# A hand-fixed order of issue in place of a planner, and weight loads issued by ScalarE

## The chip, the core and the metric

The kernel runs on one core of a Trainium2 chip. The metric is the device time of that core in microseconds, lower being better. A core has five engines that run their own instruction streams in order: TensorE (PE) for matmuls, VectorE (DVE), ScalarE (ACT) and GpSimd (POOL) for elementwise work, and SyncE (SP), which here only starts DMA transfers. An engine waits only for the semaphores that its next instruction names. PSUM is the memory that TensorE writes into, in banks; SBUF is the memory that everything else works in.

## What is computed

First a linear attention with decay over 768 steps, for 4 batches of 8 heads of width 48, then a feed-forward layer on the 384 columns that the heads make together.

```
state = 0                                   # [B, H, 48, 48]
for t in range(768):
    cur   = (u * k[t]) outer v[t]
    y[t]  = r[t] @ (state + cur)
    state = w * state + k[t] outer v[t]

x   = y, heads joined to 384 columns        # 4 x 768 rows
xn  = (x - mean(x)) / sqrt(var(x) + 1e-6) * g_ln
out = x + relu(xn @ w_ch1) @ w_ch2          # 384 -> 1536 -> 384
```

## The kernel before

The rows are cut into 24 tiles of 128 (six to a batch). The recurrence is computed by chunks of 128 steps: inside a chunk as a masked matrix of scores, between chunks by a running state. A tile i goes through these steps, and the names below are those of the tasks in the code:

- loads: `k{i}`, `v{i}`, and `r{e}` for a pair of tiles, all from HBM;
- `sck{i}`, `scr{e}0`, `scr{e}1`: k and r multiplied by tables of powers of the decay (`Fk`, `Fr0`, `Fr1`);
- `TK{i}`, `TR{e}` on PE transpose them into the PSUM bank "tr"; `kT{i}`, `rT{i}` copy the results to SBUF; `vc{i}` casts v;
- `q{i}`, `cc{i}`, `cp{i}`, `Vb{i}`: the bonus term with u, as a factor on v;
- `at{i}` on PE gives the scores, `A{i}` on DVE masks them, `y{i}` on PE multiplies by v and adds what comes from the state;
- `kv{i}`, `S{i}`, `Z{i}`: the state for the next tile, which `WLZ` (a spread table of the decay over a chunk) multiplies;
- `x{i}`, `xn{i}`, `sq{i}`, `rs{e}`: the tile of x with its sum, centered, its squares, and one over the standard deviation;
- `ln{i}` (transposed on PE for tiles 0 to 7) and `lc{i}` (its copy to SBUF, or a DMA transpose from tile 8 on) give the transposed input of the feed-forward layer;
- `up{g}_{m}` on PE multiplies by w1 into one of two "hp" banks, `re{g}_{m}` applies relu; a group g is one tile for the first six and two tiles after that, with 3 or 6 ups;
- `dn{i}0` to `dn{i}2` on PE multiply by the three thirds of w2 into bank "o"; `ot{i}` scales and adds x; `st{i}` stores. The last tile is done in two halves of the columns (`dh`, `oh`, `sh`).

The weights come as three thirds each: `w1l0` to `w1l2` and `w2l0` to `w2l2`, 768 KB apiece, in float32. `w1s{n}{kc}` casts w1 and multiplies it by minus `g_ln` (the table `g_neg`, task `gn`); `w2s{n}{f}` casts w2. An up with m = 0, 1, 2 of a single-tile group needs the third with the same number, and so does a down third.

Every step is a task with an engine, sometimes with other engines that could do it (`alt`), the tasks that it needs, and the buffers that it takes and gives. The method `order` of the class `Planner` plays a list schedule: it keeps a clock for each engine, picks the task that can start first by its assumed costs and lags, breaks ties by priority, and picks the engine that would end it first. A table `SHIFT` changes priorities, earliest times and engines of 24 tasks by name. The instructions are emitted in the order that comes out, and each engine's stream has just that order. Where the plan foresees a gap on PE before the first down matmul, `keep_warm` fills it with matmuls of an identity matrix into a spare bank (line 285), whose results nobody reads.

In this kernel SP starts nearly all DMAs, the weights among them (`load_w1`, line 234, and `load_w2`, line 238). ACT starts the first v and six stores. DMAs started by SP share one hardware queue, those by ACT another. Each DMA signals on one of eight semaphores, and a DMA that is given a semaphore in use waits at its issue until the earlier DMA on it has landed.

Of the kernel before, what the change touches and what calls it, by code (L numbers as in the profile page):

```python
# [22 lines left out]
SHIFT = {  # L23
    "up9_0": (0.0, 94.5, ""), "S15": (-4.2, 0.0, ""), "cp14": (0.0, 81.3, ""), "ln5": (0.0, 43.7, ""),
    "re12_4": (0.0, 131.8, ""), "Vb2": (0.0, 25.0, ""), "dn52": (-5.3, 0.0, ""), "q19": (0.0, 103.6, ""),
    "xn16": (0.0, 0.0, "DVE"), "x17": (0.0, 99.3, ""), "sq15": (0.0, 89.8, ""), "sck3": (0.0, 18.7, ""),
    "dn32": (7.3, 0.0, ""), "y10": (0.0, 67.0, ""), "v13": (0.0, 52.8, ""), "TR2": (0.0, 27.7, ""),
    "w1l0": (0.0, 11.3, ""), "v9": (0.0, 40.3, ""), "re7_1": (0.0, 73.1, ""), "Vb19": (0.0, 107.1, ""),
    "rT5": (0.0, 0.0, "DVE"), "re13_1": (0.0, 0.0, "DVE"), "re9_1": (0.0, 0.0, "ACT"), "q21": (0.0, 114.6, ""),
}  # L30


class Planner:
# [12 lines left out]
    def add(self, name, eng, cost, fn, needs=(), takes=(), gives=(), pri=0, load=0.0, kind=None,  # L46
            alt=None, lands=1.9, after=0.0):

        t = dict(name=name, eng=eng, cost=cost, fn=fn, needs=list(needs), takes=list(takes),
                 gives=list(gives), pri=pri, load=load, kind=kind, alt=alt, lands=lands, end=None,
                 first=(eng, cost), after=after)
        self.tasks.append(t)
        assert name not in self.by_name, name
        if name in SHIFT:
            p, late, e = SHIFT[name]
            t["pri"], t["after"] = pri + p, max(after, late)
            for other in [t["first"]] + (alt or []):
                if other[0] == e:  # L60
                    t["first"], t["only"] = other, True
        self.by_name[name] = t

    def order(self, patience=0.0, spread=0.0, seed=0):


        rng = random.Random(seed)
        family = {t["name"]: t["name"].rstrip("0123456789_") for t in self.tasks}
        vary = {f: rng.uniform(-spread, spread) for f in sorted(set(family.values()))}
        for t in self.tasks:  # L70
            t["end"] = None
            t["eng"], t["cost"] = t["first"]
        free_at = {k: [0.0] * n for k, n in self.room.items()}
        held = {}
        eng_at = {e: 0.0 for e in self.LAG}
        eng_at["SP"], dma_at = 3.5, 5.9
        last_kind = None
        todo = list(self.tasks)
        out = []
        while todo:  # L80
            best = None
            for t in todo:
                data = t["after"]
                ok = True
                for n in t["needs"]:
                    d = self.by_name[n]
                    if d["end"] is None:
                        ok = False
                        break
                    lag = 0.0 if d["eng"] == t["eng"] else self.LAG[d["eng"]]  # L90
                    if d["load"] and d["lands"] == 1.9 and t["eng"] and d["start"] > SLT:
                        lag += SLK
                    data = max(data, d["end"] + lag)
                if not ok:
                    continue
                for b, _, _ in t["takes"]:
                    if not free_at[b]:
                        ok = False
                        break
                    data = max(data, min(free_at[b]))  # L100
                if not ok:
                    continue
                pri = t["pri"] + vary[family[t["name"]]]
                if t["kind"] is not None and t["kind"] == last_kind:
                    pri -= 0.5
                pick = None
                for eng, cost in [(t["eng"], t["cost"])] + ([] if "only" in t else t["alt"] or []):
                    ready = max(data, eng_at[eng] if eng else 0.0)
                    if t["load"]:
                        ready = max(ready, dma_at - (3.0 if eng == "SP" else 2.0))  # L110
                    if pick is None or ready + cost < pick[0]:
                        pick = (ready + cost, ready, eng, cost)
                key = (pick[1] - (patience * pri if pick[2] in ("DVE", "ACT", "POOL") else 0.0), -pri)
                if best is None or key < best[0]:
                    best = (key, t, pick)
            assert best is not None, [t["name"] for t in todo][:20]
            t, (_, t0, eng, cost) = best[1:]
            t["eng"], t["cost"] = eng, cost
            todo.remove(t)
            if t["kind"] is not None:  # L120
                last_kind = t["kind"]
            end = t0 + t["cost"]
            if t["eng"]:
                eng_at[t["eng"]] = end
            if t["load"]:
                dma_at = max(dma_at, end + 1.2) + t["load"]
                end = dma_at + t["lands"]
            t["start"], t["end"] = t0, end
            for b, owner, uses in t["takes"]:
                slots = free_at[b]  # L130
                slots.remove(min(slots))
                held[b, owner] = [uses, 0.0]
            for b, owner in t["gives"]:
                h = held[b, owner]
                h[0] -= 1
                h[1] = max(h[1], end)
                if h[0] == 0:
                    free_at[b].append(h[1] + self.LAG[t["eng"]])
            out.append(t)
        return out  # L140
# [3 lines left out]
def kernel(  # L144
# [82 lines left out]
    NW = 3  # L227
# [4 lines left out]
    def load_w1(n):  # L232
        w1_f[n] = wst.tile([P, CK, FW], FP32, name="wst")
        nc.sync.dma_start(out=w1_f[n][:], in_=w1_src[:, n])  # L234

    def load_w2(n):
        w2_f[n] = wst.tile([P, FK // NW, C], FP32, name="wst")
        nc.sync.dma_start(out=w2_f[n][:], in_=w2_src[:, n * FK // NW : (n + 1) * FK // NW])
# [44 lines left out]
    def keep_warm(n):  # L283
        for _ in range(n):
            nc.tensor.matmul(out=warm[:, :P], lhsT=ident[:], rhs=ident[:], start=True, stop=True)  # L285
# [318 lines left out]
    xT_t, hT_t, o_t, rs_t, sum_s = {}, {}, {}, {}, {}  # L604
# [8 lines left out]
    LNP = 8  # L613
    KP = 24
    SZ, QP = 6, 8
    ot_t = {}

    def ln_transposes(i):
        g, j = tile_group[i]
        if g not in xT_t:  # L620
            xT_t[g] = sb3.tile([P, CK, GW], BF16, name="xT")
        tp_t[i] = ps.tile([P, 2 * HP, P], BF16, name="tr")
        for kc in range(CK):
            nc.tensor.transpose(
                out=tp_t[i][:, kc, :], in_=xn_t[i][:, kc * P : (kc + 1) * P], identity=ident[:]
            )
# [7 lines left out]
    def ln_evacuate(i, eng):  # L634
        g, j = tile_group[i]
        (eng.copy if eng is nc.scalar else eng.tensor_copy)(out=xT_t[g][:, :, j * P : (j + 1) * P], in_=tp_t[i][:, :CK, :])
# [123 lines left out]
    for rank, (a, i) in enumerate(seq):  # L760
        pri = 50 - 0.1 * rank
        if a == "w1l":
            add(f"w1l{i}", "SP", 0.6, lambda i=i: load_w1(i), takes=[("wst", ("w1", i), CK)], pri=pri, load=2.1)
        elif a == "w2l":
            add(f"w2l{i}", "SP", 0.6,
# [15 lines left out]
    for i in range(NT):  # L781
# [5 lines left out]
        add(f"sckb{i}", "", 0.0, None, [], [("sck", i, 1 if last else 2)], pri=p0)  # L787
        add(f"sck{i}", "DVE", 0.7, lambda e, i=i: scale_k(i, e), [f"k{i}", "Fk", f"sckb{i}"], [], [("k", i)], pri=p0, after=35 + (i - 6) * PACE if i > 6 else 0.0,
            alt=[("POOL", 1.0)])
        if not half:  # L790
            add(f"scrb{e}", "", 0.0, None, [], [("scr", e, 1)], pri=p0)
# [58 lines left out]
        if i < LNP:  # L850
            add(f"ln{i}", "PE", 0.18, lambda i=i: ln_transposes(i), [f"xn{i}", f"xT{g}"], [("tr", ("l", i), 1)],
                [("xn", i)], pri=p0 + 2)
            add(f"lc{i}", "ACT", 0.5, lambda e, i=i: ln_evacuate(i, e), [f"ln{i}"], [], [("tr", ("l", i))], pri=p0 + 2, alt=[("DVE", 0.36)])
        else:
            add(f"lc{i}", "SP", 1.2, lambda i=i: ln_by_dma(i), [f"xn{i}", f"xT{g}"], [], [("xn", i)], pri=90, load=0.5, lands=3.0)
# [29 lines left out]
    pe_at = 6.3  # L885
    for t in plan.order():
        if t["eng"] == "PE":
            gap = t["start"] - pe_at - 0.1
            if gap > 0 and 0 not in o_t:
                keep_warm(int(gap / 0.057))  # L890
            pe_at = t["start"] + t["cost"]
        if t["fn"] is not None:
            if t["alt"] is not None:
                t["fn"]({"ACT": nc.scalar, "DVE": nc.vector, "POOL": nc.gpsimd, "SP": nc.sync}[t["eng"]])
            else:
                t["fn"]()
# [28 lines left out]
```

## Time and profile before

| | us |
|---|---|
| median of 11 runs | 157.91 |
| lowest and highest of them | 156.77, 159.8 |
| the profiled execution, own time | 157.31 |
| the profiled execution, span of the core | 155.2 |

The span runs from the first to the last instruction of the core in the trace; some 2 us of the measured time lie outside it. The profile page gives, for each engine, the time in which it was busy and its share of the span, then the span in 40 slices. It follows the chain of work that ended last back from the end, and prints its shares. Groups of instructions stand under the line of the code that issued them; "idle before" is the time that the engine stood still just before the instructions of the group, with the one that ended the wait. A matmul record includes the time until its result is out, so consecutive matmuls overlap in the records, and the spacing of their starts is what counts. "SPq" is the time that SP's sequencer spent issuing DMAs. In the timeline each line gives the start, the duration, the engine, the line of code, the operation, output and input, and how many instructions are merged.

### The profile page before, as it was taken

The page shows a single profiled execution, that of the slowest core. Times are in us where ns is not written, and L with a number is a line of the kernel's source. Part 1 is how long each engine was busy: PE and PEld are TensorE (multiplying, and loading weights), DVE is VectorE, ACT ScalarE, POOL GpSimd, SP SyncE. Part 2 cuts the span into 40 slices and gives each one's busy share as a digit, 9 for nine tenths or more (in the row PEclk, how much of TensorE's full clock was granted, in tenths as well). Part 3 has the DMA queues.
Part 4 walks back from the last instruction along what each step waited for, and adds up shares of the span by engine and source line. Part 5 has one row for each costly group of instructions (what it writes and reads, how often), then busy time and mean ns, then how long its engine had stood idle before and what let it go on. Part 6 is the DMA issues. An engine that isn't in the chain of part 4 may idle for free.

```text
span 155.2 us, 4730 instructions
## 1 busy us (share of the span) xinstructions
PE 147.8 (95%) x1902; PEld 118.2 (76%) x1902; DVE 120.4 (78%) x246; ACT 93.6 (60%) x205; POOL 84.7 (55%) x115
## 2 busy tenths in 40 slices
PE   5999989979999999999999999999999999999991
PEld 5879988968878668677777877778787787777670
DVE  5989589599999999999799987988988965111141
ACT  3474788487887767868675677658576452444100
POOL 7397659388378866996789764963432702000000
PEclk9999999999999999999999999999999999999999
DMA  4999999999999999899597995512212112111122
GB/s 95 230 229 327 358 203 293 367 192 189 250 210 218 233 246 220 195 207 244 149 195 173 190 190 146 160 25 78 80 25 80 51 25 80 51 51 51 55 101 101
DMA packets 75563, 25.48 MB, mean 164 GB/s; under 512 B 69648, under 2 KB 74390, under 8 KB 75542
## 3 DMA queue, kind: packets, MB, share of 16 engines
q1 hardware_dynamic: 73542, 23.90, 63.9%
q10 hardware_dynamic: 1904, 1.28, 2.6%
q8 instruction: 15, 0.25, 0.7%
q14 instruction: 6, 0.05, 0.1%
q0 software_dynamic: 96, 0.01, 0.0%
HBM read 18.88 MB, written 4.72 MB: 152 GB/s over the span
## 4 chain that ended last, share of the span: by engine, by line
PE 69%; SPq 14%; DVE 7%; DMA 5%; issue 2%; ACT 1%; DVEq 0%
PE o L676 26%; PE hp L649 24%; SPq L212 8%; DMA wst<-in_moe_w_ch_dram 5%; PE at L444 3%; SPq L206 3%; PE y L547 3%; PE tr L420 2%; PE tr L405 2%; SPq L234 2%; PE y L535 2%; PE s L495 2%; PE s L464 2%; PE hp L708 1%; PE hp L676 1%
## 5 line engine op out<-in xcount | busy, mean ns | idle before, releaser
L649 PE MATMUL hp<-xT,w_sb 128*128 128x256 bf16 (+1 forms) x540 | 57.6, 251 | 0.0
L676 PE MATMUL o<-w_sb,hT 128*128 128x384 bf16 x264 | 52.3, 326 | 0.0
L663 ACT ACTIVATE hT<-hp 128x512 bf16<-128x512 f32 x62 | 36.4, 595 | 23.8 <-PE hp L649 23.1
L649 PEld LDWEIGHTS <-w_sb 128*128 128x128 bf16 x540 | 43.5, 98 | 7.3
L676 PEld LDWEIGHTS <-hT 128*128 128x128 bf16 x276 | 25.4, 98 | 11.7
L454 DVE TENSOR_TENSOR A<-at,mask 128x1024 bf16<-128x1024 f32 x24 | 29.1, 1214 | 1.5 <-PE at L444 1.4
L479 POOL TENSOR_TENSOR Vb<-v,cc 128x384 f32<-128x384 f32 x24 | 21.2, 884 | 11.4 <-ACT cc L475 6.6
L686 DVE SCALAR_TENSOR_TENSOR ot<-o,rs,x 128x384 f32<-128x384 f32 x22 | 13.4, 611 | 15.4 <-PE o L676 15.2
L390 POOL TENSOR_TENSOR sc<-r,Fr 128x384 bf16<-128x384 f32 x15 | 16.3, 1094 | 3.8 <-DVE Fr L330 2.8
L387 POOL TENSOR_TENSOR sc<-k,Fk 128x384 bf16<-128x384 f32 x16 | 16.9, 1058 | 0.0
L587 ACT ACTIVATE sq<-x,sum 128x384 bf16<-128x384 f32 x24 | 14.7, 611 | 3.4 <-DVE x L560 2.1
L285 PE MATMUL o<-ident 128*128 128x128 bf16 x191 | 14.3, 230 | 1.6 <-DVE ident L260 1.6
L409 ACT COPY kT<-tr 128x512 bf16<-128x512 bf16 x22 | 12.8, 584 | 4.1 <-PE tr L405 2.7
L560 DVE SCALAR_TENSOR_TENSOR x<-y,Vb 128x384 f32<-128x384 f32 x24 | 13.2, 549 | 1.9 <-PE y L547 1.9
L285 PEld LDWEIGHTS <-ident 128*128 128x128 bf16 x191 | 12.0, 103 | 1.9 <-DVE ident L260 1.6
L426 ACT COPY rT<-tr 128x512 bf16<-128x512 bf16 x16 | 11.2, 738 | 2.7 <-PE tr L420 2.6
L598 POOL TENSOR_SCALAR rs<-sqs 128x2 f32<-128x2 f32 x12 | 2.5, 210 | 17.8 <-ACT sq L587 17.4
L444 PE MATMUL at<-rT,kT 48*128 48x128 bf16 x192 | 9.5, 218 | 1.0 <-DVE rT L426 0.7
L574 DVE TENSOR_SCALAR xn<-x,sum 128x384 bf16<-128x384 f32 x17 | 9.9, 585 | 0.1
L405 PE MATMUL tr<-ident,sc 128*128 128x128 bf16 x92 | 8.9, 219 | 0.8 <-DVE rT L426 0.6
L665 DVE TENSOR_SCALAR hT<-hp 128x512 bf16<-128x512 f32 x10 | 6.9, 687 | 3.0 <-PE hp L649 2.9
L601 POOL TENSOR_TENSOR rs<-rs,expo 128x2 f32<-128x2 f32 x12 | 8.6, 717 | 1.0
(93 smaller groups left out, 204.4 us busy)
## 6 DMA issues: line engine op xcount, KB each, us to landing
r<-in_r_dram SPq DMA_DIRECT2D x12, 384.0 KB, 5.0
k<-in_k_dram SPq DMA_DIRECT2D x24, 192.0 KB, 4.5
wst<-in_moe_w_ch_dram SPq DMA_DIRECT2D x6, 768.0 KB, 7.4
v<-in_v_dram SPq DMA_DIRECT2D x23, 192.0 KB, 4.2
out_dram<-ot SPq DMA_DIRECT2D x18, 192.0 KB, 2.1
out_dram<-ot ACTq DMA_DIRECT2D x5, 192.0 KB, 1.9
xT<-xn SPq DMA_TRANSPOSE x16, 2.8
v<-in_v_dram ACTq DMA_DIRECT2D x1, 192.0 KB, 3.8
```

The lines of the kernel that those rows point to most:

```text
L285: nc.tensor.matmul(out=warm[:, :P], lhsT=ident[:], rhs=ident[:], start=True, stop=True)
L387: eng.tensor_tensor(out=k_bufs[i % NSC][:, :, :D], in0=k_t[i][:], in1=Fk[:], op=ALU.mult)
L390: eng.tensor_tensor(out=r_bufs[e % NSR][:, j, :, :D], in0=r_t[e][:, :, j * D : (j + 1) * D], in1=Fr[:, j], op=ALU.mult)
L444: nc.tensor.matmul(out=at_t[i][:, par, p, :], lhsT=kT_t[i][p0 : p0 + D, p, :], rhs=rT_t[i][p0 : p0 + D, p, :], start=True, stop=True,)
L454: nc.vector.tensor_tensor(out=A_t[i][:].rearrange("p e q t -> p (e q) t"), in0=at_t[i][:].rearrange("p e q t -> p (e q) t"), in1=mask[:].u ...
L479: nc.gpsimd.tensor_tensor(out=Vb_t[i][:], in0=vf_t[i][:], in1=cc_t[i][:].unsqueeze(2).to_broadcast([P, H, D]), op=ALU.mult)
L560: nc.vector.scalar_tensor_tensor(out=x_t[i][:], in0=y_t[i][:, :C], scalar=1.0, in1=Vb_t[i][:].rearrange("p h d -> p (h d)"), op0=ALU.mult, ...
L587: nc.scalar.activation(out=sq[:], in_=x_t[i][:], func=ACT.Square, bias=sum_t[i][:], scale=-float(C), accum_out=sq_t[e][:, c : c + 1],)
L649: nc.tensor.matmul(out=hp[:, f * gw : (f + 1) * gw], lhsT=w1_sb[:, n, kc, fb * P : (fb + 1) * P], rhs=xT_t[g][:, kc, :gw], start=(kc == 0) ...
L663: nc.scalar.activation(out=out, in_=src, func=ACT.Relu)
L676: nc.tensor.matmul(out=o_t[i][:, :C], lhsT=hT_t[g][:, fk, j * P : (j + 1) * P], rhs=w2_sb[:, fk, :], start=(fk == 0), stop=(fk == FK - 1),)
L686: nc.vector.scalar_tensor_tensor(out=ot_t[i][:], in0=o_t[i][:, :C], scalar=rs_t[i // 2][:, i % 2 : i % 2 + 1], in1=x_t[i][:], op0=ALU.mult ...
```

## The change

The planner's `order` no longer plans. It reads a constant text `ORDER`, over 800 names in one sequence for the whole program, each with the letter of the engine where there is a choice (A for ACT, V for DVE, G for POOL, S for SP), and emits the tasks so. An entry such as `*12` asks for that many filler matmuls; the text asks for 53 of them, besides the 22 that stand outside the plan in both kernels. `SHIFT` is gone. `load_w1` and `load_w2` are issued by ACT. The transposes `ln0` to `ln3` go to bank "o", which is unused before the first down matmul, instead of bank "tr". The tasks `sckb` and `scrb`, which stand for the hand-rotated buffers of scaled k and r and issue no instruction, now name the tasks that read the buffer before.

```diff
-SHIFT = {
-    "up9_0": (0.0, 94.5, ""), "S15": (-4.2, 0.0, ""), "cp14": (0.0, 81.3, ""), "ln5": (0.0, 43.7, ""),
...
-}
+ORDER = """
+k1.S Fr0.V r1.S v1.S k2.S Fk.A Fr1.A scr01.G sck1.G scr00.V sck0.V *16 TK0 *4 TR0 v2.S k3.A scr11.G kT0.V scr10.G
+*1 turn vec uw.V rT0.A *20 at0 vc0.A w1l0 rT1.V TK1 wl kT1.A vc1.A w1l2 q1.G q0.V A0 cc0 *12 TR1 kv0 at1 sck2.V
+cp0.V Vb0 sck3.G WLZ Z0 A1 gn cc1 y0 kv1 rT3.A rT2.A TK2 kT2.A r2.S cp1.V Vb1 x0 w1s02.A xn0.A vc2.G w1l1 Z1 y1
+w1s01.G q2.V at2 x1 xn1.A cc2 kv2 TK3 kT3.A v3.S cp2.V sq0 A2 Vb2 w1s00.G ln1 lc1.V w1s20.A w1s21.G k4.S y2 at3
+ln0 lc0.A w1s22.V up1_0 re1_0.A up0_2 re0_2.A up1_2 k5.S Z2 re1_2.A x2 xn2.V q3.V ln2 scr20.G scr21.G cc3 TR2 A3
+vc3.V up0_0 rT4.V lc2.A w1s11.G v4.S cp3.V w2l0 up2_0 kv3 re2_0.V w1s12.G w1s10.G re0_0.A rT5.A sck4.V Vb3 up2_2
+re2_2.A w2l1 up0_1 sq1 re0_1.A TK4 y3 Z3 sck5.G up2_1 re2_1.A w2l2 kT4.V at4 vc4.G q4.G up1_1 x3 xn3.V cc4 ln3
+TK5 lc3.A sq2 w2s01.A w2s02.A kv4 A4 y4 re1_1.V cp4.V kT5.V w2s03.V Z4 up3_2 re3_2.A w2s00.V up3_0 rs0 Vb4 x4
+xn4.V r3.S q5.G at5 w2s13.G up3_1 cc5 dn00 v5.S re3_0.A ln4 k6.S w2s20.G w2s12.V w2s10.A re3_1.A w2s11.V dn01
+w2s23.A w2s22.A lc4.V cp5.A up4_2 re4_2.A A5 w2s21.V up4_0 dn02 scr31.G scr30.V up4_1 ot0 Vb5 r4.S re4_0.A vc5.V
...
+"""
...
-    def order(self, patience=0.0, spread=0.0, seed=0):
...
+    def order(self):
...
+        for word in ORDER.split():
+            if word[0] == "*":
+                out.append(dict(warm=int(word[1:])))
+                continue
+            name, _, eng = word.partition(".")
+            t = self.by_name[name]
+            if eng:
+                t["eng"] = {"P": "PE", "A": "ACT", "V": "DVE", "G": "POOL", "S": "SP"}[eng]
...
     def load_w1(n):
         w1_f[n] = wst.tile([P, CK, FW], FP32, name="wst")
-        nc.sync.dma_start(out=w1_f[n][:], in_=w1_src[:, n])
+        nc.scalar.dma_start(out=w1_f[n][:], in_=w1_src[:, n])
 
     def load_w2(n):
         w2_f[n] = wst.tile([P, FK // NW, C], FP32, name="wst")
-        nc.sync.dma_start(out=w2_f[n][:], in_=w2_src[:, n * FK // NW : (n + 1) * FK // NW])
+        nc.scalar.dma_start(out=w2_f[n][:], in_=w2_src[:, n * FK // NW : (n + 1) * FK // NW])
...
+    LNO = 4
...
+    def ln_bank(i):
+        return "o" if i < LNO else "tr"
...
-        tp_t[i] = ps.tile([P, 2 * HP, P], BF16, name="tr")
+        tl_t[i] = ps.tile([P, 2 * HP, P], BF16, name=ln_bank(i))
...
-        add(f"sckb{i}", "", 0.0, None, [], [("sck", i, 1 if last else 2)], pri=p0)
+        add(f"sckb{i}", "", 0.0, None, ([f"TK{i - NSC}"] + ([f"kv{i - NSC}"] if (i - NSC) % NCH < NCH - 1 else [])) if i >= NSC else [], [("sck", i, 1 if last else 2)], pri=p0)
...
     for t in plan.order():
-        if t["eng"] == "PE":
-            gap = t["start"] - pe_at - 0.1
-            if gap > 0 and 0 not in o_t:
-                keep_warm(int(gap / 0.057))
-            pe_at = t["start"] + t["cost"]
...
+        if "warm" in t:
+            keep_warm(t["warm"])
```

In the new order the engines of some tasks differ from what the planner chose. On DVE there are 24 relus instead of 10, 9 `xn` instead of 17, 4 halves of `scr` instead of 9, 12 `Z` instead of 15, 5 `rT` instead of 8 and 7 `kT` instead of 2. POOL does 20 halves of `scr` instead of 15, 8 `Z` instead of 5, 12 casts of v instead of 10 and 6 scalings of w1 instead of 3. ACT does 48 relus instead of 62 and starts the six weight loads, three of the k, three more of the v, and eight stores of tiles instead of five. The TensorE stream holds the same useful matmuls, in another sequence: twelve ups stand ahead of `dn00` where six did.

## The prediction

> **What bounds the kernel now.** I read the page's head, engine rows and chain first, then ten-microsecond windows, then the timeline of the first 37 us.
>
> ```profile
> span 155.2 us, 4730 instructions
> PE 147.8 (95%) x1902; PEld 118.2 (76%) x1902; DVE 120.4 (78%) x246; ACT 93.6 (60%) x205; POOL 84.7 (55%) x115
> DMA  4999999999999999899597995512212112111122
> ...
> PE 69%; SPq 14%; DVE 7%; DMA 5%; issue 2%; ACT 1%; DVEq 0%
> ...
> L285 PE MATMUL o<-ident 128*128 128x128 bf16 x191 | 14.3, 230 | 1.6 <-DVE ident L260 1.6
> ```
>
> TensorE looks full, but 14.3 us of it is the filler of L285. The SPq and DMA shares of the chain are the first 31 us: loads end last there. After that the chain is TensorE, with a stretch of VectorE between 56 and 66 us. The windows say why:
>
> ```profile
> 10.00:20.00 10.00, 9.98 (x193) 9.54 (x192) 7.93 (x19) 6.61 (x15) 7.04 (x10) 1.00 1.06 313
> 40.00:50.00 10.00, 10.00 (x167) 8.55 (x165) 9.67 (x18) 7.71 (x18) 6.76 (x8) 1.00 0.99 218
> 60.00:70.00 10.00, 9.70 (x132) 7.42 (x130) 9.91 (x20) 6.78 (x15) 9.57 (x12) 1.00 0.96 202
> 120.00:130.00 10.00, 10.00 (x105) 7.66 (x103) 7.16 (x14) 4.78 (x10) 4.19 (x6) 1.00 0.22 66
> ```
>
> Columns: PE, PEld, DVE, ACT, POOL, clock, DMA share, GB/s. Early the DMA engines have no free time; from 40 to 70 us VectorE (9.67, 9.91) is as full as TensorE; late, only TensorE is.
>
> ```profile
> 9.81 3.17 SPq L234 DMA_DIRECT2D wst<-in_moe_w_ch_dram  x3
> 15.65 1.65 POOL L371 TENSOR_SCALAR w_sb<-wst,g_neg 128x512 bf16<-128x512 f32 x2 [1.04 <-DMA wst<-in_moe_w_ch_dram]
> 22.08 1.75 SPq L238 DMA_DIRECT2D wst<-in_moe_w_ch_dram  x3
> 25.02 4.62 SPq L206 DMA_DIRECT2D r<-in_r_dram  x1
> 33.40 0.50 POOL L381 CAST w_sb<-wst 128x384 bf16<-128x384 f32 x1 [0.35 <-DMA wst<-in_moe_w_ch_dram]
> ```
>
> The first up matmul is at 17.26 us and the first down matmul at 29.41, each just behind its weights. The last w2 third was there at about 33.4.
>
> I then counted TensorE's useful work by issue spacing, from the chain (0.65 for a down third, 0.67 for a single-tile up, 0.33 for scores) and the timeline (TK 0.22, TR 0.45, cc 0.10, kv 0.17 to 0.32, y 0.20 to 0.37, ln 0.16). 72 ups are 47.4 us, 69 downs 44.9, 6 half downs 2.0, attention and transposes 34.5: 128.8 in all, the same in both kernels. The span is 7.2 before the first transpose + 128.8 + gaps + 3.3 after the last matmul (151.97), so gaps are 15.9. Position in the work tells where: dn00 starts at 29.41 with 11.4 done, 10.8 of gap since 7.2; TR3 at 37.03 with 17.7 done, 1.3 more; at 55.80 35.5 is done, 1.0 more; then 2.8 to the end. So the prize is the start, and about 3.8 us later.
>
> **What the Trainium skill says.** "DMA: Bandwidth & Descriptors", section "Issuing engines are not separate DMA queues": DMAs of all issuers run on the same 16 engines; another issuer saves only issue time. The DMA row agrees in that the early slices are full with one queue. Its section "Queues, rings and completion order" says that the engines alternate between queues packet by packet, so weights from ScalarE no longer wait behind SyncE's k, v and r; how the shares fall, the trace before hardly shows. "TensorE: Matmul & The Clock Gate", section "Part 1: The HAM clock gate": after an idle window of some 3.4 us the array runs at half rate until it was busy as long. The trace agrees at the start: 12 fillers at 1.61 us take 1.46 us, 22 at 6.05 take 1.39. Section "Architectural detail" of that page: ScalarE and VectorE are strict FIFOs, which makes a wait at a load's issue stop what follows.
>
> **The change part by part.**
> *Weights.* Six issues leave SP; ACT gets them, and three k, three v, three stores and one half store more than before. An ACT issue took 0.45 in the trace (v0). 16 x 0.45 = 7 us of ACT sequencer time, against 14 relus fewer (8.3 us) and other shifts: ACT stays near level.
> *Completion semaphores.* Each DMA of the built program also waits for an earlier DMA on the same one of eight semaphores. In the new order w1l2 (ACT) waits for v2, r3 (SP) for w2l1 and v5 (SP) for w2l2; k6, r4, k7 and v6 stand behind v5.
> *Start, walked in the order listing with the durations above.* v2 lands near 13.5 (in before its packets ended near 11.2; here k3 and w1l0 share the engines). ACT holds at w1l2 until then, so WLZ ends near 14.7 (11.7 before) and Z0, A1, g_neg follow on VectorE: g_neg near 16.7 (11.8 before). VectorE then has Z0, A1, gn, cp1, x0, Z1, q2, x1, cp2, A2, lc1 = 6.3 us without a break: lc1 near 21. GpSimd's w1s00 is last in a row of 1.0-us scalings: 21.3. So the first up is near 21.9 instead of 17.26. But filler (191 matmuls down to 75) goes with it: at 21.9 the old order had 6.4 done, the new one 5.6. That costs 0.9.
> *Middle.* The new order runs 12 ups, not 6, before dn00 (17.1 of work ahead of it, 11.4 before). ACT from 24.7: lc2, w2l0 (25.2), re0_0, rT5, re2_2, w2l1 (27.9), sq1, re0_1, re2_1, w2l2 (30.4), each by its row. An issue to first packet took 1.35 for v0, the packets of a w2 third some 2.25, landing 1.5 more (w1: packets end near 14.1, used at 15.65): w2l2 at 35.5, later than the 33.4 of before. VectorE reaches w2s21 near 37.5; dn02 37.7; TR3 39.0. v5, issued at 35.5, lands 3.9 later (3.8 for v0, median 4.2 for v), its cast takes 0.35: y5 near 39.9 with 21.7 done. The old order had 21.7 done at 41.1. Gain 1.2.
> *Next.* k6, r4, k7, v6 land near 40, 42, 43, 44; their users stand at 42 to 46. Walking on to y7 (31.0 done) gives 49.5: 0.4 of gap more, as before.
> *Rest.* VectorE loses 8 xn (0.585), 5 scalings of r (0.81), 3 Z (0.8), 3 rT (0.73) and takes 14 relus (0.69), 5 kT (0.41). Counted by place, the stretch from 16 to 96 us of work holds 82.5 us of VectorE rows, 86.3 before: 3.8 less, scaled by 120.4 busy over 129.9 summed: 3.5 less; the relus move behind 104. GpSimd gains 12 us (5 r scalings, 3 Z, 2 casts, 3 w1), with room: 65 in those 80. The old kernel had 3.4 of gaps from 31.0 on; I take 1.0 of that away, bounds 2.5 (most of it was VectorE) and -1.5 (fixed orders stall at their own places, for instance up14_0, whose lc22 hangs on y22 at 105.5 of work, 6.6 later than in the old order).
> *LayerNorm transposes 0 to 3 in bank o* free bank tr; they wait on lc1's 0.36 only: nothing. *Added needs of sckb and scrb* carry no instruction.
> *Clock.* With filler ending near 12.7 TensorE is idle up to 2.6 us at a time until 21.9. If it drops to half rate there, bounds are 0 and 1.7 us (half of 3.4). I take 0: no wholly idle window of 3.4.
> Sum: 1.2 + 1.0 = 2.2 less. Span 153.0. The profiled execution took 157.31, 2.1 more than its span: 155.1. It lies 0.6 under the median of 157.91, so on that footing 155.7.
>
> **The rivals.**
> *Slower: in-order ACT holds the weights back.* Each w2 issue stands behind relus that wait for TensorE, and SP behind the w2 landings; every microsecond that w2l2 is late moves y5. Half clock until 25 (+1.5), issues at 0.5 to 1.8 each as SP's w1 took (+0.6 x 3), shared engines (+0.9) make w2l2 39.7: +4.2, so 159.9. It decides once w2l2 lands after 37.7. For: ACT is walked full from 24.7 to 30.4. Against: SP's own issues slowed only with a full queue.
> *Larger gain: VectorE was the later bound.* Then 2.5 of later gaps go: 154.2. For: 9.91 in 60 to 70; against: TensorE idled only 0.3 there.
> *No change:* the half clock costs 1.5 and the later gaps stay: 157.9 to 158.3. For: the filler is missing; against: the idle times are short.
> That the edit does nothing is excluded: the listings differ from the start.
>
> **How the numbers follow.** Forecast 155.7, chance 0.33, own range 154.8 to 157.1; larger gain 0.20; no change within 0.5%, which is what a measurement of this kernel tells apart, 0.13; slower 0.34. Faster 0.53. The range goes from 153.0 (larger gain with all 2.5 and a prompt w2l2) to 160.2.
>
> **What would show it.** First up near 22, WLZ near 14.7, L285 down to 75, w2l2's casts at 35 to 36, y5 near 40, fewer VectorE gaps from 55 to 80. Wrong if ups before 30 take 1.3 each, if w2l2 is used after 37.7, or if TensorE shows gaps of over a microsecond after 50.

## The result and the profile after

The changed kernel took 160.98 us (median of 12 runs, 159.94 to 161.46); the kernel before took 157.9 (47 runs, 156.28 to 163.58). The ratio is 1.0211, with a 95% interval of 1.0183 to 1.024: slower by 3 us where 2.2 us less were forecast, and outside the range given. The profiled execution of the changed kernel took 161.4, its span is 159.6. Ratios here and below are taken over undisturbed runs alone and medians over all, so the two need not agree to the last half per cent.

The page of the changed kernel, with the same rows as were shown of before and its row of clocks added:

```profile
span 159.6 us, 4489 instructions
...
PE 145.3 (91%) x1786; PEld 113.8 (71%) x1786; DVE 124.4 (78%) x251; ACT 84.2 (53%) x188; POOL 94.0 (59%) x127
...
PEclk9999857999999999999999999999999999999999
DMA  3999999992299794698299937970181062121023
...
PE 56%; DVE 24%; POOL 8%; DMA 3%; issue 3%; ACT 2%; SPq 1%; POOLq 0%; DVEq 0%; ACTq 0%
```

And its filler, from the list of TensorE's groups:

```profile
L261 PE MATMUL o<-ident 128*128 128x128 bf16 x75 | 6.5, 246 | 1.6 <-DVE ident L236 1.6
```

Filler went from 14.3 to 6.5 us, yet TensorE's busy time fell by 2.5 only. The chain has moved: SyncE's queue, 14% before, is at 1%, and VectorE and GpSimd, 7% before, hold 32% of it. The DMA row, full to the 19th slice before, shows holes at the tenth and eleventh slice.

Three signs stand in the windows (PE, PEld, DVE, ACT, POOL busy, clock, DMA share, GB/s):

```profile
20.00:30.00 10.00, 9.23 (x126) 8.58 (x125) 8.69 (x15) 5.79 (x12) 8.79 (x11) 0.71 1.06 264
...
60.00:70.00 10.00, 9.28 (x114) 6.73 (x112) 8.89 (x18) 6.36 (x14) 8.05 (x9) 1.00 0.63 152
...
120.00:130.00 10.00, 9.17 (x108) 6.78 (x106) 6.86 (x16) 6.70 (x16) 3.66 (x6) 1.00 0.20 61
```

From 20 to 30 us TensorE looks busy, at 0.71 of its clock. From 60 to 70 us VectorE is relieved as forecast (8.89, before 9.91), and TensorE idles more, not less (9.28, before 9.70). From 120 to 130 us no engine is full, where TensorE was at 10.00 before.

Next, lines of the changed kernel's timeline (start, us, what). SyncE:

```profile
20.25 0.69 SPq L182 DMA_DIRECT2D r<-in_r_dram  x1
20.99 3.04 SPq L188 DMA_DIRECT2D v<-in_v_dram  x1
...
27.12 1.52 SPq L188 DMA_DIRECT2D v<-in_v_dram  x1
42.06 0.37 SPq L680 DMA_DIRECT2D out_dram<-ot  x1
```

SyncE issued r3 at 20.25, v5 at 20.99 and v6 at 27.12, and then stood at the first store until 42.06: that is the hole in the DMA row. ScalarE:

```profile
31.89 0.38 ACTq L214 DMA_DIRECT2D wst<-in_moe_w_ch_dram  x1
...
39.47 0.93 ACT L357 CAST w_sb<-wst 128x384 bf16<-128x384 f32 x2 [1.02 <-DMA wst<-in_moe_w_ch_dram]
```

It issued the last third of w2 at 31.89, came to its casts before the data (1.02 us idle) and cast at 39.47. TensorE:

```profile
22.43 3.74 PE L632 MATMUL hp<-xT,w_sb 128*128 128x128 bf16 x36
...
41.77 0.61 PE L396 MATMUL tr<-ident,sc 128*128 128x128 bf16 x8
```

The first three ups (36 matmuls) took 3.74 us; in e6 below the same 36 took 2.35. TR3 began at 41.77.

To find where the time goes I took each TensorE task's start less the useful work done before it. Where this offset grows, time is lost. In us, for 8, 12, 22, 43, 80 us of work and at the end:

| kernel | 8 | 12 | 22 | 43 | 80 | end |
|---|---|---|---|---|---|---|
| before | 15.73 | 18.00 | 19.38 | 20.48 | 22.58 | 23.04 |
| after | 18.45 | 19.08 | 20.54 | 23.06 | 24.79 | 27.39 |

At 22 us of work (TR3) the change is 1.16 behind. It loses 1.42 more up to 43, nothing up to 80 (in fact 0.37 comes back), and 2.14 in the rest. The whole loss of this table, 4.35, is more than the 3.1 between the medians, because the traced execution of before was one of its shorter ones (157.31) and that of the change one of its longer ones (161.4); single traces show places, and the ratios below show sizes. The last part is two gaps, which TensorE's timeline names (in brackets the idle time before, and who ended it):

```profile
107.13 0.33 PE L471 MATMUL s<-vv,sc 128*128 128x96 bf16 x4 [0.92 <-ACT cc L451]
...
121.19 0.81 PE L632 MATMUL hp<-xT,w_sb 128*128 128x256 bf16 x6 [0.83 <-ACT hT L646]
```

and ScalarE's timeline at the first of them says what ScalarE was doing:

```profile
104.46 0.60 ACT L554 ACTIVATE xn<-x,sum 128x384 bf16<-128x384 f32 x1
106.32 0.73 ACT L402 COPY rT<-tr 128x512 bf16<-128x512 bf16 x1 [1.25 <-DVE rT L402]
106.91 0.17 ACT L451 COPY cc<-s 128x8 f32<-128x8 f32 x1
```

It waited. cp18 (the 0.17-us copy) had its operand from 105.54, but it stands behind rT21, and rT21 waited 1.25 us for VectorE's rT20. At 121 us re11_5 stands in the same way behind cp20, sq16 and rT22.

### The profile page after: what moved, and what is told of

It is laid out like the page before. It is cut to its first block, busy times and chain, and to the rows that moved or that the text cites. A ratio compares the mean times of both kernels' runs of the same rounds, so it can differ in the third digit from the quotient of the medians.

```text
span 159.6 us, 4489 instructions
## 1 busy us (share of the span) xinstructions
PE 145.3 (91%) x1786; PEld 113.8 (71%) x1786; DVE 124.4 (78%) x251; ACT 84.2 (53%) x188; POOL 94.0 (59%) x127
## 3 DMA queue, kind: packets, MB, share of 16 engines
q10 hardware_dynamic: 11504, 7.87, 17.1%
## 4 chain that ended last, share of the span: by engine, by line
PE 56%; DVE 24%; POOL 8%; DMA 3%; issue 3%; ACT 2%; SPq 1%; POOLq 0%; DVEq 0%; ACTq 0%
PE hp L632 22%; PE o L659 19%; DVE A L430 5%; DMA k<-in_k_dram 3%; PE at L420 3%; DVE sc L363 2%; POOL Vb L455 2%; PE tr L381 2%; POOL sc L363 2%; PE y L523 2%; DVE x L536 2%; DVE ot L669 2%; DVE w_sb L357 2%; DVE xn L550 2%; DVE hT L648 2%
## 5 line engine op out<-in xcount | busy, mean ns | idle before, releaser
L659 PE MATMUL o<-w_sb,hT 128*128 128x384 bf16 x264 | 53.7, 326 | 0.4 <-DVE w_sb L357 0.3
L646 ACT ACTIVATE hT<-hp 128x512 bf16<-128x512 f32 x48 | 28.3, 597 | 22.7 <-PE hp L632 22.6
L648 DVE TENSOR_SCALAR hT<-hp 128x512 bf16<-128x512 f32 x24 | 16.3, 686 | 11.8 <-PE hp L632 11.5
L366 POOL TENSOR_TENSOR sc<-r,Fr 128x384 bf16<-128x384 f32 x20 | 20.7, 1040 | 3.6 <-ACT Fr L306 3.3
L402 ACT COPY rT<-tr 128x512 bf16<-128x512 bf16 x19 | 13.4, 737 | 11.2 <-PE tr L396 9.2
L385 ACT COPY kT<-tr 128x512 bf16<-128x512 bf16 x17 | 9.9, 584 | 14.3 <-PE tr L381 9.0
L563 ACT ACTIVATE sq<-x,sum 128x384 bf16<-128x384 f32 x24 | 14.7, 616 | 0.0
L554 ACT ACTIVATE xn<-x,sum 128x384 bf16<-128x384 f32 x15 | 9.2, 614 | 6.2 <-DVE x L536 6.2
L495 POOL TENSOR_TENSOR Z<-S,WLZ 128x384 bf16<-128x384 f32 x8 | 8.0, 998 | 6.6 <-DVE S L486 6.6
L381 PEld LDWEIGHTS <-sc 128*128 128x128 bf16 x96 | 6.7, 100 | 4.9 <-DVE sc L363 2.1
L523 PE MATMUL y<-vv,A 128*128 128x48 bf16 x192 | 8.8, 185 | 0.3 <-DVE A L430 0.3
```

Source lines behind the costliest of these rows:

```text
L366: eng.tensor_tensor(out=r_bufs[e % NSR][:, j, :, :D], in0=r_t[e][:, :, j * D : (j + 1) * D], in1=Fr[:, j], op=ALU.mult)
L381: nc.tensor.transpose(out=tk_t[i][:, q, :], in_=sc[:, q, :], identity=ident[:])
L563: nc.scalar.activation(out=sq[:], in_=x_t[i][:], func=ACT.Square, bias=sum_t[i][:], scale=-float(C), accum_out=sq_t[e][:, c : c + 1],)
L646: nc.scalar.activation(out=out, in_=src, func=ACT.Relu)
L648: nc.vector.tensor_scalar(out=out, in0=src, scalar1=0.0, scalar2=None, op0=ALU.max)
L659: nc.tensor.matmul(out=o_t[i][:, :C], lhsT=hT_t[g][:, fk, j * P : (j + 1) * P], rhs=w2_sb[:, fk, :], start=(fk == 0), stop=(fk == FK - 1),)
```

## The experiments

The table gives the result of every run. Each ratio is to the kernel before on the same chip. "Fixed" is the changed kernel's order. The text of the order is wrapped anew in some runs, so that their line numbers are two or three lower.

| run | order, weights' queue, what else | us | ratio, 95% |
|---|---|---|---|
| the change | fixed, ACT | 160.98 | 1.0211 (1.0183 to 1.024) |
| e1 | fixed, ACT, 40 fillers | 161.2 | 1.0175 (1.0149 to 1.0201) |
| e2 | fixed, SP | 160.72 | 1.0112 (1.005 to 1.0175) |
| e3 | planner's, ACT | 164.29 | 1.0384 (1.032 to 1.0447) |
| e4 | fixed, ACT, first store later | 161.49 | 1.0199 (1.0154 to 1.0243) |
| e5 | e1 with the store later | 162.22 | 1.0293 (1.0245 to 1.0342) |
| e6 | fixed, ACT, two late places moved | 158.98 | 1.0101 (1.0062 to 1.0141) |
| e7 | e5 with w2's loads earlier | 171.43 | 1.0898 (1.0846 to 1.0949) |
| e8 | e7 with VectorE relieved | 172.35 | 1.0937 (1.0887 to 1.0986) |
| e9 | fixed, SP, two late places moved | 158.31 | 0.9994 (0.9962 to 1.0026) |
| e10 | e9 with VectorE relieved | 157.75 | 1.0004 (0.9966 to 1.0041) |
| e11 | e10 with 40 fillers | 159.67 | 1.0126 (1.007 to 1.0182) |
| e12 | planner's, ACT, w1 four places earlier | 166.95 | 1.0543 (1.0457 to 1.0629) |
| e13 | e9 with uw on GpSimd | 158.46 | 0.9956 (0.992 to 0.9993) |
| e14 | e6 with w1 on SP | 158.71 | 1.0051 (1.0025 to 1.0077) |
| e15 | e6 with w2 on SP | 157.95 | 0.9993 (0.9959 to 1.0027) |

**The clock (e1).** Forty more matmuls without use between 14 and 20 us keep the clock at full rate.

```diff
-kv0 at1 sck2.V ... kT2.A r2.S ... at2 x1 ... cc2 kv2 TK3
+kv0 at1 *16 sck2.V ... kT2.A *14 r2.S ... at2 *6 x1 ... cc2 kv2 *4 TK3
```

> The changed kernel with 40 filler matmuls put back in four places between at1 and TK3 (16 after at1, 14 after kT2, 6 after at2, 4 after kv2). Theory clock (the array fell to half rate from about 19 to 26 us because filler is missing): the clock row shows no slice under 9 between 15 and 27 us, the first three ups take 0.67 each and not some 1.2, dn00 starts 1.0 to 1.5 us earlier than 36.85, and the time is 159.5 to 160.0. Rival VectorE (its own chain of work from 10 to 45 us sets the start, whatever the array does): the clock is whole, but dn00 moves by less than 0.4 us and the time stays within 0.4 of 160.98.

dn00 came 2.17 us earlier (34.68, in the change 36.85), more than the clock theory had, and yet the time stayed where its rival had it. The clock was whole (0.997 in this run) and the offset at 22 us of work fell from 20.54 to 18.52, but it rose by 1.88 at one later place, and the end came at 27.22 instead of 27.39. TensorE's timeline shows the place:

```profile
52.05 0.33 PE L471 MATMUL s<-vv,sc 128*128 128x96 bf16 x4 [1.72 <-ACT vv L372]
```

This is kv7, whose vv7 waited on GpSimd until 51.5 for v7, one of the loads that start in a burst once SyncE is past the first store. Of the 2.02 us at the start, 1.32 were there at 4 us of work already, before the clock had fallen (a row of VectorE that varies, see e13 and the last section), so that 0.7 is left for the clock; e10 and e11, which differ by fillers alone, give about 1 in the same way. Either way the end did not see it. That fillers bring nothing does not show that the half rate costs nothing, since the fillers take TensorE's time too and moved other work: of the twelve executions of e10, the eight with a mean clock of 0.988 or more took 156.89 to 157.94 us, the four with 0.967 to 0.978 took 158.91 to 159.3. What makes them differ is not taken apart.

**The store (e4, e5).** The first store is moved behind other loads on SyncE: behind k12 in e4, behind k9 with e1's fillers in e5.

```diff
-dn11 sck6.G st0.S ln5 ... kv6 k9.S Z6
+dn11 sck6.G ln5 ... kv6 k9.S st0.S Z6
```

> The changed kernel with the first store (st0) moved in SyncE's stream from ahead of v8 to behind k12, so that v8, k9, v9, r5, r6 and k12 no longer stand behind a store that waits for ot0 until 42.06 us. Theory head of line (SyncE issued nothing from 28.6 to 42.06 us and the loads of tiles 8 to 12 came late, which makes the gaps of 1.4 us from 47 to 62 us): time 159.6 to 160.4, those loads issued before 36 us. Rival (GpSimd and VectorE are the bound from 46 to 62 us, the loads are there in time): within 0.4 of 160.98; or slower, if these loads share the DMA engines with the w2 thirds and make the last one land after 40 us.

> The kernel after with the 40 filler multiplies of the first run (clock kept whole to 20 us) and, besides, the first store moved on SyncE's queue behind k9's load. Theory that the 2 us won at the start were lost again to chunk 7's v, which landed at 51.5 us because SyncE stood at the store of ot0 from 31 to 39.8 us: the wait of POOL for v7 (2.2 us) and of TensorE for vv7 (1.7 us) go, the offset stays under 20.5 at 34 us of work, the time falls to 159.0 to 159.6. Rival, that VectorE's and GpSimd's strings of work set the pace between 25 and 60 us: v7 is early and the time stays at 160.8 to 161.3. Third possibility: the loads let through early share the engines with w2 and w2l2 lands after 38.5, the loss then sits at dn02 instead.

In e4 v8, k9 and v9 were issued by 34 us, r5, r6 and k12 still at 40 or later, and the time did not move: 1.0199 is the change's own ratio within the intervals. In e5 POOL's wait for v7 fell from 2.2 to 0.9 us and the offset at 43 us of work from e1's 22.92 to 22.42. But the time did not fall. The trace is of the shortest of its four executions, and the median is 1.3 us above that. Neither theory's number came, and why the median rose is open. That the burst behind the store was worth 2 us is refuted.

**The queue alone (e2, e3).** One word in `load_w1` and `load_w2`: back to SyncE in the fixed order (e2), and to ScalarE in the planner's order of before (e3).

```diff
-        nc.scalar.dma_start(out=w2_f[n][:], in_=w2_src[...])
+        nc.sync.dma_start(out=w2_f[n][:], in_=w2_src[...])
```

> The changed kernel with the six weight loads issued by SyncE again, at the same places of the order. Theory weights (the w2 thirds come late because ScalarE issues them behind its relus while SyncE runs ahead with r3 to v6 on the same DMA engines; w2l2 was used at 39.5): the last w2 cast starts near 35 to 37 us and the time is 158.5 to 160.3. Rival: the order, not the queue, makes the loss; then the last w2 cast moves but the time stays within 0.5 of 160.98, or grows because SyncE now holds the later k, v and r behind the weights.

> The kernel before, its planned order of issue unchanged, with only the six weight loads issued by ScalarE. Theory order (the queue costs little by itself, the fixed order costs nearly all): within 0.6 us of 157.91. Theory weights: slower by 1 to 3 us, 159 to 161, with the first up later than 17.26 us or the last w2 cast later than 33.4 us.

The queue costs in both orders, 1.0% in the fixed one and 3.8% in the planner's. e2's 160.72 lies within its rival's half microsecond of 160.98, but the kernel before took 158.66 beside it, so the ratios decide, 1.0112 against 1.0211. The sign that its theory named did not come: the last cast of w2 began at 39.49 (in the change 39.89), though the data had landed at 32.53, because VectorE came to it no sooner. e3 lost more than either of its numbers. Its first up starts at 22.57 instead of 17.26 and its first down at 37.60 instead of 29.41. ScalarE's and TensorE's timelines say why:

```profile
15.54 0.38 ACTq L234 DMA_DIRECT2D wst<-in_moe_w_ch_dram  x1
15.95 0.51 ACT L396 CAST vv<-v 128x384 bf16<-128x384 f32 x1 [4.12 <-DMA v<-in_v_dram]
...
20.80 0.48 PE L624 MATMUL tr<-ident,xn 128*128 128x128 bf16 x3 [4.16 <-ACT kT L409]
...
24.70 1.48 PE L649 MATMUL hp<-xT,w_sb 128*128 128x128 bf16 x12
```

ScalarE idled 4.12 us, until a v had landed, and then issued w1's second third; the cast behind it only shows the wait. TensorE then stood 4.16 us for ScalarE's copies, and its clock fell: the 12 matmuls of an up took 1.48 us, later 0.83. How much of the 3.8% each of the two is was not taken apart. The transfers of this program signal on eight semaphores in turn, counted over both queues, and an issue waits until the transfer eight before it in the program has landed. On SyncE, which only issues transfers, such a wait can hold back nothing but transfers. On ScalarE it holds copies that TensorE waits for.

**The two late places (e6).**

```diff
-x17 rT21.A cc18 r11.S scr111.G dn120 cp18.A Vb18
+x17 cc18 r11.S scr111.G dn120 cp18.A rT21.A Vb18
-re11_3.V cp20.A cc21 st11.S sq16 rT22.A re11_5.A rT23.A
+re11_3.V re11_5.A cp20.A cc21 st11.S sq16 rT22.A rT23.A
```

> The kernel after with two places of ScalarE's order changed: cp18 ahead of rT21 (chunk 18's cc no longer waits for VectorE's rT20), re11_5 ahead of cp20. If the two late stalls (kv18 at 107.1, 0.92 us; up11_1 at 121.2, 0.83 us) are losses of the order alone, with nothing else late behind them, both go and the time falls by 1.5 to 2.1, to 158.9 to 159.5. Rival: another operand is late at the same places (A19 behind VectorE's work, hp's buffers) and no more than 0.5 comes back.

As the theory had it: 158.98 was measured. Neither gap is left, and between 80 us of work and the end the offset grows by 0.56 instead of 2.60. In ScalarE's timeline of this run cp18 comes first:

```profile
104.77 0.17 ACT L448 COPY cc<-s 128x8 f32<-128x8 f32 x1 [0.57 <-PE s L437]
105.45 0.74 ACT L399 COPY rT<-tr 128x512 bf16<-128x512 bf16 x1 [0.52 <-DVE rT L399]
```

rT21 still waits for VectorE, and nobody waits for rT21.

**w2 earlier on ScalarE (e7, e8).** The three issues of w2 are put forward in ScalarE's order; e8 adds xn2 to xn5, re1_1 and w2s03 on ScalarE in place of VectorE.

```diff
-w1l1 Z1 ... w1s20.A ... up1_0 re1_0.A
+w1l1 w2l0 Z1 ... w1s20.A w2l1 ... up1_0 re1_0.A w2l2
```

> As the run with fillers and the store moved, and besides w2's three loads issued earlier on ScalarE's queue (behind w1l1, w1s20 and re1_0: about 17, 21 and 22 us instead of 23, 28 and 30). Theory that the weights' place in ScalarE's order holds dn00 to dn02: w2l2 lands at 33 to 35 instead of 37.5, dn02 starts before 37.5, and the time falls by another 0.5 to 1.5 against that run. Rival, that the transfers fill the engines whatever their order and the work that waits for k4, v4 and r3 pays: w2 is early, but the second to fifth chunks are later and the time stays within 0.5 of that run or rises.

> As the run with w2 early, and besides xn2 to xn5, re1_1 and w2s03 on ScalarE instead of VectorE. Theory that VectorE's unbroken string of work (20 to 42 us) sets the pace there, its SBUF-to-SBUF rows lengthened beside GpSimd: 4 us of VectorE's rows go, 1 to 2 us come back against the run with w2 early, 157.0 to 158.5. Rival: ScalarE in its fixed order becomes late in its place (re and rT behind xn), no gain or a loss up to 1.

They lost 14 and 15 us against before, 9 and 10 against e5, far outside what either theory had. ScalarE's timeline of e7:

```profile
22.55 0.71 ACT L343 ACTIVATE w_sb<-wst,g_neg 128x512 bf16<-128x512 f32 x1
29.72 0.37 ACTq L212 DMA_DIRECT2D wst<-in_moe_w_ch_dram  x1
30.13 0.48 ACT L617 COPY xT<-o 128x384 bf16<-128x384 bf16 x1 [6.87 <-DMA v<-in_v_dram]
```

The issue of w2's second third held ScalarE for 6.87 us, until a v had landed. The program's list of waits has that too:

```
27 L212 DMACopy wst<-in_moe_w_ch_dram 128x4x384 [waits DMAHW2_49,Activation_49,Pool_49]
```

Activation and Pool are the buffer's last readers. DMAHW2 is a transfer's semaphore, last given to v5, which comes much later in the list of tasks, but stands before w2l1 in the built program, because SyncE runs ahead. The relief of VectorE could not be read behind such a hold, so it was tried again on SyncE's queue (e10).

**Both repairs together (e9), and what more VectorE or the clock give (e10, e11).**

> The fixed order with both repairs so far: the weights' loads back on SyncE's queue, and ScalarE's two late places changed (cp18 ahead of rT21, re11_5 ahead of cp20). If the loss of the change is the sum of independent parts, the ratio to before is 1.011 (weights on SyncE) less the 2.0 us of the late stalls, 0.998 to 1.002: no loss left. Rival: the parts overlap, as the clock's did, and the ratio stays at 1.006 or more.

> As the run with both repairs, and xn3, xn4, re1_1, w2s03, w2s11 and w2s21 on ScalarE instead of VectorE. Theory that VectorE's string of work from 20 to 38 us, its copies lengthened beside GpSimd, is what dn01 and dn02 wait for once the weights are on SyncE (TensorE waited 1.5 us at dn01 and 1.2 at dn02 with w2 landed by 32): 1.5 to 3 us come back, ratio 0.980 to 0.990. Rival: ScalarE's order makes the same casts as late there, ratio within 0.004 of the run with both repairs.

> As the run before it, with the 40 filler multiplies between 14 and 20 us that keep the clock whole. If the start is bound by TensorE's clock, another 1 to 2 us; if it is bound by VectorE's string of work, which the clock doesn't change, within 0.5 of the run without fillers, as it was in the first run with fillers. I take the second.

e9 is level with before, as the sum of independent parts had it. e10's rival is right: taking six rows from VectorE moved nothing. The fillers made it slower by 1.2% (five executions, and an interval from 0.7% to 1.8%), which neither side of that expectation had. The two traces don't show where, for they end alike (spans of 157.2 and 157.0 us, with a mean clock of 0.967 in e10's, one of its four at a lower clock, and 1.0 in e11's); why is open.

**w1 earlier in the planner's order (e12).**

```diff
-    N1, N2 = 9, 14
+    N1, N2 = 5, 14
```

> The planner's order of before with the weights on ScalarE's queue, as in the earlier run of it (1.038), but w1's loads placed four loads earlier in the planner's list, so that what each of them waits for before it may be issued (the landing of the transfer eight before it in the program) is over sooner. Theory that ScalarE, held at these issues, is what cost: w1's third load is issued before 15 us instead of 18.6, the first up starts at 18 to 21 us instead of 27.6, and at least 5 of the 8 us come back, ratio 0.995 to 1.010. Rival: the two queues' transfers share the engines and this is what made w1 late, the first up stays after 24 us and the ratio over 1.025.

The 27.6 in this expectation is wrong: e3's first up is at 22.57. Half of the theory came true. w1's third load was issued at 11.32, and the first up started at 17.58, as early as in before. The time rose all the same, and the timeline shows that the hold had moved to w2's first issue:

```profile
27.04 0.38 ACTq L238 DMA_DIRECT2D wst<-in_moe_w_ch_dram  x1
27.46 0.60 ACT L663 ACTIVATE hT<-hp 128x512 bf16<-128x512 f32 x1 [4.10 <-DMA v<-in_v_dram]
```

The first down began at 36.93, hardly before e3's 37.60. The planner also made a new order for everything after, so the rest of this loss is not taken apart.

**Which weights (e14, e15).** One word each, from e9.

> The fixed order with the two late places mended, w1's loads on SyncE's queue, w2's on ScalarE's. All on ScalarE was 1.0101, all on SyncE 0.9994. Theory A, that w1 on ScalarE costs (it stands at w1's second issue until v2 has landed, kT1 and WLZ behind it): 0.998 to 1.003 here. Theory B, that w2 on ScalarE costs (issued in its place in the order, sharing the engines with r3 to v6, landing at 39): 1.006 to 1.012 here.

> The counterpart: w1's loads on ScalarE's queue, w2's on SyncE's, the late places mended. Theory A: 1.006 to 1.012. Theory B: 0.998 to 1.003. If both this and its counterpart lie near 1.005 the loss is shared between the two.

w1 alone on ScalarE's queue costs nothing (0.9993 beside 0.9994). w2 alone costs 0.57%, both together 1.07%. So w2 is what costs (theory B), though e14 came just under the number for it. ScalarE's casts of w2's last third in e14 and e15:

```profile
38.04 0.93 ACT L354 CAST w_sb<-wst 128x384 bf16<-128x384 f32 x2 [2.89 <-DMA wst<-in_moe_w_ch_dram]
```

```profile
35.35 0.92 ACT L354 CAST w_sb<-wst 128x384 bf16<-128x384 f32 x2
```

On SyncE the data were there when ScalarE came to them. On ScalarE's queue the engine waited 2.89 us, and GpSimd 3.09 for the same data. But this wait is not what reaches TensorE: the last down third of the first tile starts at 38.82 in e14 and at 39.84 in e15, where TensorE had waited 1.46 us at the second one for a cast of data that had long landed. What the traces show is an effect behind it. In e14:

```profile
38.07 0.70 POOL L354 CAST w_sb<-wst 128x384 bf16<-128x384 f32 x1 [3.09 <-DMA wst<-in_moe_w_ch_dram]
...
41.86 0.99 POOL L363 TENSOR_TENSOR sc<-r,Fr 128x384 bf16<-128x384 f32 x1
42.15 0.91 DVE L547 TENSOR_SCALAR xn<-x,sum 128x384 bf16<-128x384 f32 x1
43.12 0.34 PE L604 MATMUL tr<-ident,xn 128*128 128x128 bf16 x3 [0.38 <-DVE xn L547]
```

and in e15:

```profile
38.78 0.99 POOL L363 TENSOR_TENSOR sc<-r,Fr 128x384 bf16<-128x384 f32 x1
42.89 0.42 DVE L547 TENSOR_SCALAR xn<-x,sum 128x384 bf16<-128x384 f32 x1
```

GpSimd, late by its wait for w2, comes to its scaling of r just when VectorE is at xn5, which then takes 0.91 us instead of 0.42 (the last section has a like case), and TensorE waits for it at ln5. All six traces of the fixed order with w2 on ScalarE in its first place (the change, e1, e4, e5, e6, e14) have xn5 at 0.90 to 0.92 and TensorE waiting 0.37 to 0.39 there; all six with w2 on SyncE (e2, e9, e10, e11, e13, e15) have 0.42 and no wait. That is 0.4 to 0.5 of the 0.9 to 1.7 us that the queue costs; where the rest lies is open. That w1 adds to the loss only when w2 is there too fits w2's issues being later behind later ups (the first at 24.64 in e6, 23.66 in e14), but the intervals of e6 and e14 overlap, so there may be nothing to explain; it was not tested by itself.

**A small row on VectorE (e13).**

```diff
-k3.A scr11.G kT0.V scr10.G *1 turn vec uw.V rT0.A
+k3.A kT0.V *1 turn vec uw.G scr11.G scr10.G rT0.A
```

> The fixed order with both repairs (0.9994 to before), and besides the two small products uw (4 columns each) on GpSimd, ahead of scr11 and scr10, instead of on VectorE. In the run with the weights on SyncE the pair took 1.98 us on VectorE beside GpSimd's rows and rT1, q0 and A0 stood behind it; in before it took 0.33. Theory that this is a loss of the start: rT1 starts at 9.6 to 9.8 instead of 10.7 to 11.6, TK1 1 to 2 us earlier, and 0.5 to 1.5 us come back in all, ratio 0.990 to 0.997. Rival: cc0 and TR1 wait for what GpSimd then does later (scr11, scr10), or the start is hidden as with the fillers: ratio 0.998 to 1.003.

The ratio is 0.9956 with an interval that ends at 0.9993, at the weak end of the theory. TK1 started at 10.84, where it started at 11.00 to 12.49 in the runs of the fixed order with uw on VectorE. It is the one version whose interval lies ahead of before, by 0.4%, but that interval overlaps e9's and it is one of fifteen tried, so it is hardly a gain one can rely on.

## Why the prediction was wrong

*Start.* The numbers came out, and by luck. WLZ ended at 14.49 (forecast 14.7), g_neg at 16.7 to 17.1 (16.7), and the first up began at 22.43 (21.9). The forecast had ScalarE held at w1l2 until v2 lands. w1l2 was issued at 13.08, but it held nothing up:

```profile
12.88 0.58 ACT L385 COPY kT<-tr 128x512 bf16<-128x512 bf16 x1 [2.14 <-PE tr L381]
13.08 0.38 ACTq L210 DMA_DIRECT2D wst<-in_moe_w_ch_dram  x1
13.36 0.52 ACT L372 CAST vv<-v 128x384 bf16<-128x384 f32 x1
13.78 0.71 ACT L337 COPY WLZ<-wl 48x192 f32<-48x192 f32 x2
```

ScalarE went from kT1 to WLZ without a pause, and kT1 waited for TensorE's TK1, which waited 1.09 us for rT1, which stood on VectorE behind the pair uw: 1.50 us here, priced at 0.33 from before. In e2, where ScalarE issues no weights, WLZ ends at 14.50 and the first up starts at 22.06, and in e15 w1 on ScalarE's queue cost nothing.

*Completion semaphores.* This step failed, in its direction. It had SyncE's r3 and v5 waiting for w2's second and third part. The trace has r3 issued at 20.25 and v5 at 20.99, ten microseconds before those parts. The built program gives semaphores in the order in which its transfers stand, with SyncE far ahead, so it is w2l1 that waits for r3, and w2l2 for v5. In the changed kernel these waits were over in time (r3 landed at 26.44, v5 at 27.32, and w2l1 was issued at 29.96). In e3, e7 and e12 such waits held ScalarE for 4.1, 6.9 and 4.1 us.

*w2's landing.* From that followed the mis-sized term of the middle. With SyncE taken to be standing, w2l2 was given the engines to itself, 5.1 us from issue to use (30.4 to 35.5). In fact it was issued at 31.89 and cast at 39.47, 7.6 us. r3, v5, k6 and r4 had landed by then (the last at 31.32), but k7 and v6 landed at 33.05 and 33.85, and w2l1, ahead of it on the same queue, at 37.42. So 1.5 of the 4.0 us is the later issue and 2.5 the longer way. A transfer was no slower for being on ScalarE's queue: the thirds took 5.5 to 7.6 us from issue to landing, in e9 on SyncE's queue 5.9 to 10.4. What the queue changed is the issue, 26.38 to 31.89 where e9 has 22.80 to 24.11. The first rival named this, each issue behind relus that wait for TensorE, with 39.7 and the point from which it decides, 37.7. It was given 0.34 and is what happened, but it was sized at 4.2 us against the forecast, where the runs give w2's queue 0.57% (e9 to e14) to 1.08% (e15 to e6), 0.9 to 1.7 us: with w2 landed by 31.4 to 34.3, VectorE still came to its last cast at 36.6 to 39.5 (e2, e9, e13, e15). With the half clock's share in it, the gain of 1.2 at TR3 became a loss of 1.16.

*Next and rest.* This step failed most. It took 1.0 off the later gaps because 3.5 us of VectorE rows leave. From 22 us of work to the end the gaps were 6.85 instead of before's 3.66, so 3.2 more. VectorE was relieved, as the window from 60 to 70 us shows, yet TensorE idled more there, and where e10 relieved it further, between 25 and 38 us, nothing came of it. "Fixed orders stall at their own places" stood there as a bound of 1.5 only, with the place guessed wrong (up14_0). The places were kv18 and up11_1, worth 1.1% (the change to e6) or 1.18% (e2 to e9).

*Clock.* Taken at 0 because no idle window of 3.4 us would come. The reason was wrong: the clock fell without such a window, to 0.71 between 20 and 30 us, and it cost 0.7 to about 1 us at 22 us of work. That the price at the end was near 0 all the same was not foreseen: keeping the clock whole made the kernel no faster beyond the intervals (e1).

*The sum.* The order with two places moved and the weights on SyncE is level with before (e9). So the order itself gave none of the 1.2 us that the walk found for it. Perhaps 0.4% came back with uw (e13), within the noise of e9; relieving VectorE of six rows (e10) and fillers for the clock (e11) brought nothing. What holds the rest is open. The two places cost about 1.1%, the weights' queue about 1.0%, and together they are the change's 2.1%.

## What to carry to other kernels

A load that is moved to a computing engine's queue becomes an instruction of that engine: look up every semaphore that its issue waits for in the built program, other transfers' among them, and ask which loads the freed queue will now start earlier and put beside it. In an order fixed by hand, look for an engine that is idle with a ready copy behind a waiting one; two such places of 0.9 us cost as much here as the whole move of the weights. That an engine is full says little of what its relief is worth: try it, with the next stall in view. And a forecast that meets its number at a step is not yet right there: look at what the step waited for.

## What was not expected of the hardware

TensorE's clock fell without a long idle time. Between 10 and 22.4 us the longest gap of TensorE in the changed kernel is 1.09 us, it was busy for 6.67 us of the 10 from 10 to 20, and the clock then went to 0.71 in the ten microseconds that follow. The prediction had gone by an idle window of 3.4 us. The same page of the Trainium skill, "TensorE: Matmul & The Clock Gate", tells in its section "A second HAM failure mode: psum-queue depth-cycling" of a kernel in which short idle times between groups of matmuls were frequent enough to bring the half rate back. The gaps here (1.09, 1.09 and 0.86 us between 11 and 18 us) look alike; from which share of idle time it sets in, no run here shows. It also varies from one execution to the next: in twenty of e9 the mean clock over the span was 0.968 to 1.0.

Two products of 4 columns on VectorE took up to as long as GpSimd's rows beside them. The rows of their instructions in before, in e2, and on GpSimd in e13 (count, then least, median and longest in ns):

```profile
L351 DVE TENSOR_TENSOR uwI<-vec x2: 157/159/161, 9.2 to 9.4; 48x4 bf16<-48x4 f32 x2
```

```profile
L327 DVE TENSOR_TENSOR uwI<-vec x2: 942/985/1028, 9.6 to 10.6; 48x4 bf16<-48x4 f32 x2
```

```profile
L324 POOL TENSOR_TENSOR uwI<-vec x2: 199/201/203, 9.6 to 9.9; 48x4 bf16<-48x4 f32 x2
```

Each of the two in e2 lasts about as long as one of GpSimd's scalings beside them (two in 1.95 us, from 9.60 on), and ends with it. In e9 the first began at 9.60, the scaling at 9.62: the first took 158 ns, the second 879. In before no scaling of GpSimd stood beside the pair. The Trainium skill, "SBUF — State Buffer", section "SBUF: two separate sides", calls the pair of ports that VectorE and GpSimd share an exclusive lock, under which the later one blocks for the whole instruction; the trace agrees. The masked product A, which reads PSUM, took 1.21 and 1.22 us on the mean of its 24 in before and after, whatever GpSimd did. A change of order thus changes durations: a row priced from the trace before (0.33 for both) cost 1.98 in another place, and xn5 0.91 instead of 0.42.
